# Windowed attention with a soft mixture of experts on one core: the slot logits in four quarters of 64 tokens, some VectorE steps in other forms, and a new table of keys

## The chip, the cores and the metric

The kernel runs on one core of one Trainium2 chip, as one program. The metric is device time in microseconds (us). In three runs the kernel before took 245.77, 247.46 and 247.46 us, so its median is 247.46.

## What is computed

For 4 batches, 8 heads, 768 tokens and 64 features per head, attention keeps the 4 first keys (the sinks) and a window of 128 keys behind each query. Its output, 3072 tokens by 512 features, goes through a soft mixture of 8 experts with 4 slots each:

```
keep = is_sink | in_window                       # n_sink 4, window 128
a = softmax(where(keep, q @ k.T / 8, -1e9)); x = a @ v
logits = x @ phi                                 # [3072, 32]: 32 slots
d = softmax of logits over the 3072 tokens       # dispatch
slot_input = d.T @ x                             # [32, 512]
slot_out[e] = relu(slot_input[e] @ w1[e]) @ w2[e]   # 512 -> 1024 -> 512
c = softmax of logits over the 32 slots          # combine
return c @ slot_out                              # [3072, 512]
```

All data is float32. The weights w1 and w2 are 32 MB, in 32 tiles of 1 MB.

## The kernel before

The attention runs as 12 jobs (`window_path`, L730): 4 batches, each in 3 pieces of 256 tokens (j = 0, 1, 2). A job loads q, k and v, transposes q and k on TensorE (`prep`), and does four softmax tiles (`softmax`, L843): scores on TensorE, row maxima on VectorE (`maxima`), exponentials and row sums on ScalarE (`exps`), then the reciprocal of the sums on VectorE (`inverse`, L901) and the scaling by it on GpSimd, 128x528 elements. The weights are transposed on TensorE, the window's edges are cut by selects on GpSimd (`select`), and `values` multiplies by v. The sinks' weights go another way: they are gathered into `sk`, transposed into `pst`, and added to the logits and to the slot inputs by small matmuls.

At the end of each job `Moe.tokens` (L337) does the dispatch of its 256 tokens, once per job, so 12 times. It is an online softmax over tokens:

- `logits` (L357): 32 slots on 32 partitions, in four column groups of TensorE. Two groups hold the two blocks of 128 tokens, and the other two hold the same two blocks once more. So the tile `L` has 128 partitions and 128 columns; 16 matmuls of 128 columns, and 4 more for the sinks.
- VectorE takes the (negated) maximum of each row into `new`, and the smaller of it and the maximum so far (`tensor_tensor(new, new, old, op=ALU.min)`, L374).
- ScalarE copies the first 64 partitions as they are into `lt`, and the exponentials of the other 64 (L376, L378); their sums go to `zb`. `al`, the factor for what was summed before, is a third small step.
- TensorE turns `lt` by one 128x128 transposition; ScalarE or VectorE copies the two halves out, as `lb` (the weights) and as the logits for the combine.
- `products` (L400) multiplies the weights by the tokens, and `sums` (L419) adds that to `acc`, scaled by `al`. The sinks' part of `acc`, called `far`, has 32 columns per batch; all columns so far are scaled by `al` in each dispatch, by a `tensor_scalar` of 32 to 128 columns, and then the new product is added to the present batch's columns. `totals` (L434) does the same for the sums `z`.

`finish` (L449) joins the maxima of the partition groups, forms the slot inputs `si`, and the tail (`Moe.tail`, L588) does the experts and the combine. `slot_softmax` (L519) prepares the combine's weights once per batch.

What sets the order of the work: each step above is handed to `Plan.add` with a key, an engine and an estimate of its duration; `Plan.order` (L196) lists the steps in an order for each engine, in which the key decides among steps that could start at the same moment. The keys are the sum of 4 times the job's number and an offset from the table `CFG` (L706). The program is then written out in that order, and each engine works through its own list in that order; it is fixed before the run. All DMAs are issued from the one queue of SyncE (SP), in order.

Tiles: `Plan` hands out 4 banks of PSUM for the general tiles named `w`, and 2 larger ones for scores, named `s`. In SBUF there are 24 tiles of 1 MB named `wt` and `first`; 17 of them take weights during the attention, and the others become free for weights only when the attention's last steps have read what is in them. Nearly all instructions are recorded under one line, L156, that of the helper that issues them, so one reads them by the names of their tiles.

The lines to look at: the minimum in a dispatch

```
            plan.add(key, "V", 0.07, lambda e: nc.vector.tensor_tensor(new, new, old, op=ALU.min),
```

the scaling of the far part

```
                    nc.vector.tensor_scalar(far[:, 0:z1], far[:, 0:z1], al, None, op0=ALU.mult)
```

and the step in front of a softmax tile's reciprocal, where `eps` is a tensor

```
            nc.vector.tensor_tensor(z, z, eps, op=ALU.add)
```

Of the kernel before, what the change touches and what calls it, by code (L numbers as in the profile page):

```python
# [8 lines left out]
F32 = mybir.dt.float32  # L9
# [10 lines left out]
P = 128  # L20
# [53 lines left out]
class Sinks:  # L74


    def __init__(self, nc, plan, pool, tmp, c, v, store):
# [3 lines left out]
        self.sk = [pool.tile([P, P], F32, name=f"sk{i}") for i in range(2)]  # L81
# [16 lines left out]
        def clear(e):  # L98
            nc.gpsimd.memset(wide, 0.0)
            nc.gpsimd.memset(self.phi, 0.0)  # L100
            for t in self.sk:
                nc.gpsimd.memset(t, 0.0)
# [20 lines left out]
        plan.add(1.0, "G", 0.6, clear, w=["swide", "vphi", ("sk", 0), ("sk", 1)])  # L123
# [184 lines left out]
class Moe:  # L308
# [6 lines left out]
    def __init__(self, nc, c, keep, work, pools, B):  # L315
# [9 lines left out]
        t = keep.tile([P, 7], F32, name="sums")  # L325
        self.m, self.z, self.zb, self.al = t[:, 0:2], t[:, 2:3], t[:, 3:5], t[:, 5:7]
# [8 lines left out]
        nc.vector.memset(self.z, 0.0)  # L335

    def tokens(self, plan, keys, b, j, x, xn, blocks):  # L337
# [8 lines left out]
        old, new = self.m[:, (n + 1) % 2:(n + 1) % 2 + 1], self.m[:, n % 2:n % 2 + 1]  # L346
# [4 lines left out]
        both = len(blocks) == 2  # L351
# [4 lines left out]

        def logits(e):  # L357
            for a in range(5 if sinks else 4):
                for g in range(4):
                    if a == 4:  # L360
                        nc.tensor.matmul(L["tile"][32 * g:32 * g + 32, 0:P], lhsT=sinks.phi[:, g % 2, :], rhs=sinks.pst,
                                         start=False, stop=True, skip_group_check=True)
                        continue
                    nc.tensor.matmul(L["tile"][32 * g:32 * g + 32, 0:P], lhsT=c.phi[:, a, :],
                                     rhs=xt[:, a, x[g % 2 if both else blocks[0]]], start=(a == 0), stop=(a == 3 and not sinks),
                                     skip_group_check=True)

        plan.add(next(k), "P", 1.16 if sinks else 0.91, logits, r=xs + ["phi"] + (["pst", "vphi"] if sinks else []), w=[L["name"]], new=L, mode=(128, 32))

        key = next(k)  # L370
        plan.add(key, "V", 0.2, lambda e: nc.vector.tensor_reduce(
            new, L["tile"][:, 0:P], op=ALU.max, axis=AX.X, negate=True), r=[L["name"]], w=[("m", n % 2)])
        if n:
            plan.add(key, "V", 0.07, lambda e: nc.vector.tensor_tensor(new, new, old, op=ALU.min),  # L374
                     r=[("m", (n + 1) % 2)], w=[("m", n % 2)])
        plan.add(next(k), "A", 0.16, lambda e: nc.scalar.copy(lt[0:64], L["tile"][0:64, 0:P]), r=[L["name"]], w=["lt0"])  # L376
        plan.add(next(k), "A", 0.48,
                 lambda e: nc.scalar.activation(lt[64:128], L["tile"][64:128, 0:P], AF.Exp, bias=new[64:128],  # L378
                                                accum_out=zb[64:128]),
# [6 lines left out]
        else:  # L386
            next(k)
        plan.add(next(k), "P", 0.11, lambda e: nc.tensor.transpose(T["tile"][:, 0:P], lt, c.ident),
                 r=["lt0", "lt1"], w=[T["name"]], new=T)
        i = slice(0, 2) if both else slice(blocks[0], blocks[0] + 1)  # L390

        def natural(e, w):
            t = T["tile"][:, 0:P].rearrange("p (w i s) -> p w i s", w=2, i=2)
            o, t = (lb, t[:, 1]) if w else (lg[:, i], t[:, 0, i])
            (nc.scalar.copy if e == "A" else nc.vector.tensor_copy)(o, t)
# [4 lines left out]
        def products(e):  # L400
            for g in range(4):
                i, o = g % 2, slice(256 * (g // 2), 256 * (g // 2) + 256)
                if both:
                    lhs, rhs = lb[:, i, :], xn[i][:, o]
                else:
                    rows = slice(64 * i, 64 * i + 64)
                    lhs, rhs = lb[rows, i, :], xn[blocks[0]][rows, o]
# [11 lines left out]
        def sums(e):  # L419
            x, d = acc[:, 0:256], far[:, 32 * b:32 * b + 32]  # L420
            if sinks:
                if n:
# [11 lines left out]
        def totals(e):  # L434
            if not n:
                nc.vector.tensor_copy(z[64:128], zb[64:128])
            elif both:
                nc.vector.scalar_tensor_tensor(z[64:128], z[64:128], al[64:128], zb[64:128],
                                               op0=ALU.mult, op1=ALU.add)
            else:  # L440
                nc.vector.tensor_tensor(z[64:128], z[64:128], al[64:128], op=ALU.mult)
                nc.vector.tensor_tensor(z[64:96], z[64:96], zb[64:96], op=ALU.add)
# [4 lines left out]
        plan.add(key, "V", 0.56 if sinks else 0.4, sums, r=[S["name"], aln], w=["acc"], last=S)  # L447

    def finish(self, plan, keys):  # L449
# [4 lines left out]
        m, mo = self.m[:, (self.n - 1) % 2:(self.n - 1) % 2 + 1], self.m[:, self.n % 2:self.n % 2 + 1]  # L454
        W, Z, SI, D = plan.psum(), plan.psum(), plan.psum(), plan.psum()
        sinks = self.sinks
        f = work.tile([P, 1], F32, name="f")
# [20 lines left out]
        plan.add(next(k), "A", 0.3, lambda e: nc.scalar.activation(f, m, AF.Exp, bias=mo, scale=-1.0), r=mm, w=["f"])  # L478
# [10 lines left out]
        def far(e):  # L489
            nc.tensor.matmul(D["tile"][:, 0:64], lhsT=self.acc[:, 256:384], rhs=s2, start=True, stop=True)  # L490
# [7 lines left out]
        if sinks:  # L498
            key = next(k)
            plan.add(key, "P", 0.2, far, r=["sf", "acc"], w=["sd"], new=D)  # L500
# [18 lines left out]
    def slot_softmax(self, plan, key, b, names):  # L519
# [12 lines left out]
        def sums(_):  # L532
            nc.vector.reduce_sum(rs, e, axis=AX.X)
            nc.vector.tensor_scalar(rs, rs, EPS, None, op0=ALU.add)
            nc.vector.reciprocal(rs, rs)

        plan.add(key, "V", 0.7, sums, w=[n])
# [144 lines left out]
class Weights:  # L682
# [8 lines left out]
    def load(self, t):  # L691
# [3 lines left out]
        else:  # L695
# [10 lines left out]
CFG = {'prep': [12.62, 12.36],  # L706
       'load': [62.54, -93.04],
       'v': [68.49, 63.17],
       'S': -12.9,
       'M': 126.11,  # L710
       'E': 297.18,
       'N': -191.46,
       'K0': 89.87,
       'T': [-201.07, -298.71],
       'K': -214.45,
       'sel': [89.25, -30.52, -145.68, -195.21],
       'val': [295.22, -19.77, 342.69, 369.69],
       'xn': [-57.94],
       'tok': [357.78, -262.56, 29.9, -50.0, 133.69, -75.28, 36.37, -51.64, -299.8, 208.29, -224.86],
       'sm': -143.04,  # L720
       'sinks': -181.93,
       'tr': [63.06, 25.65, 135.89, 140.0, 109.95, 86.26, 129.98, 2.55, 42.1, 2.21, 118.89, 92.88, 82.47, 53.92,
           125.08, 116.73, 96.95, 0.0, 138.66, 84.47, 128.65, 60.63, 120.33, 77.77, 78.14, 114.47, 21.23],
       'w': [105.83, 8.0],
       'fin': [287.49, -10.46, -125.39, -132.28, 35.33, -56.83, -2.84, 389.2, -90.55, 66.83, 472.81],
       'xn1': [40.22],
       'tok1': [-9.5, -16.36, 75.49, -213.58, -107.33, 247.29, -76.98, 179.88, 150.72, 361.93, -107.59]}


def window_path(ctx, tc, c, moe, q, k, v, phi, w1, w2, out):  # L730
# [32 lines left out]
    small = t[:, 1840:1864].rearrange("p (g x y) -> p g x y", g=3, x=2)  # L763
    eps = t[:, 1864:1868]
    qt = fr.tile([P, 4, 256], F32, name="qt")
    nc.vector.memset(eps, EPS)
# [507 lines left out]
```

## Time and profile before

| | us |
|---|---|
| runs, median (lowest, highest) | 247.46 (245.77, 247.46) |
| the profiled execution, device time | 248.19 |
| its span, first to last instruction | 246.5 |
| TensorE busy (matmul) | 212.7 |
| VectorE busy | 168.9 |
| ScalarE busy | 150.4 |
| GpSimd busy | 131.7 |

The profile is one execution, so durations and stretches below are those of the run of 248.19 us; 1.69 us of it lie outside the span, and it is 0.73 us above the median of the three runs. Engines are PE (TensorE's matmuls), PEld (its weight loads), DVE (VectorE), ACT (ScalarE), POOL (GpSimd) and SP (SyncE, which issues the DMAs). A float32 matmul shows as two records. The attention takes about the first 183 us, and its jobs repeat with a period of one batch, about 43 us; the end of the last dispatch and the slot inputs follow up to 194 us, and then the experts and the combine.

### The profile page before, as it was taken

How to read it: one execution, taken by the hardware profiler on the slowest of the kernel's cores; microseconds unless marked ns; L12 is line 12 of the kernel's file. 1: busy time of each engine (PE TensorE's matmuls, PEld its weight loads, DVE VectorE, ACT ScalarE, POOL GpSimd, SP SyncE). 2: the span in 40 equal slices, each digit the busy share in tenths (PEclk: the TensorE clock that was granted, in tenths of full speed). 3: DMA queues.
4: the chain of work that ended last, by engine and by line, in shares of the span. 5: the costliest groups of instructions: out<-in, count | busy, mean ns of one | idle time of the engine just before them, and what ended most of it. 6: DMA issues, size and time to landing. Idle time of an engine off the chain costs nothing.

```text
span 246.5 us, 9008 instructions
## 1 busy us (share of the span) xinstructions
PE 212.7 (86%) x3547; PEld 151.2 (61%) x3547; DVE 168.9 (69%) x455; ACT 150.4 (61%) x579; POOL 131.7 (53%) x247
## 2 busy tenths in 40 slices
PE   7866998998979799798979998898799999998830
PEld 7754676775657577575757766576578533655520
DVE  3387896789999778999956899999736411324240
ACT  2257699758988866898886579888634212123230
POOL 3048687954777785487776646867894160000000
PEclk9979799999999999999979999999999999999995
DMA  5497997788989778998996998983119999999896
GB/s 124 104 212 168 257 212 206 287 186 244 195 251 282 229 256 174 258 198 236 278 263 195 178 274 194 311 268 134 45 44 350 419 366 357 351 349 370 297 314 214
DMA packets 102965, 59.47 MB, mean 241 GB/s; under 512 B 76292, under 2 KB 98820, under 8 KB 102916
## 3 DMA queue, kind: packets, MB, share of 16 engines
q1 hardware_dynamic: 102916, 58.83, 82.9%
q8 instruction: 30, 0.49, 0.8%
q14 instruction: 19, 0.16, 0.2%
HBM read 52.53 MB, written 6.29 MB: 239 GB/s over the span
## 4 chain that ended last, share of the span: by engine, by line
PE 50%; DVE 21%; ACT 14%; DMA 5%; issue 4%; POOL 2%; ACTq 0%; DVEq 0%; POOLq 0%
PE w L156 35%; PE s L156 14%; ACT wt L156 11%; DVE wt L156 8%; DVE s L156 7%; DMA wt<-in_moe_w_dram 5%; DVE sums L156 2%; DVE first L156 2%; PE w L1226 2%; POOL wt L156 1%; DVE acc L156 1%; DVE rs L156 1%; ACT first L156 1%; ACT wt L659 0%; ACT lt L156 0%
## 5 line engine op out<-in xcount | busy, mean ns | idle before, releaser
L156 ACT ACTIVATE wt<-s,wt 128x132 f32<-128x132 f32 x192 | 68.9, 382 | 11.0 <-PE s L156 4.6
L156 POOL TENSOR_TENSOR wt<-wt 128x528 f32<-128x528 f32 x48 | 51.2, 1066 | 28.3 <-DVE wt L156 10.0
L156 POOL TENSOR_SCALAR_AFFINE_SELECT wt<-wt 128x512 f32<-128x512 f32 x88 | 54.0, 639 | 18.8 <-ACT wt L156 12.8
L156 PE MATMUL w<-wt 128*64 128x128 f32 (+2 forms) x548 | 51.3, 324 | 4.3 <-DVE wt L156 2.6
L156 PE MATMUL s<-wt,qt 64*64 64x196 f32 (+2 forms) x768 | 44.4, 332 | 6.7 <-ACT wt L156 5.5
L156 PEld LDWEIGHTS w<-wt 128*64 128x64 f32 (+1 forms) x548 | 37.0, 144 | 16.2 <-POOL wt L156 4.4
L156 ACT ACTIVATION_READ_ACCUMULATOR wt<-s,wt 128x1 f32 x192 | 41.6, 217 | 0.0
L156 ACT COPY wt<-w 128x512 f32<-128x512 f32 (+1 forms) x50 | 28.0, 573 | 12.8 <-PE w L156 9.2
L156 DVE TENSOR_REDUCE wt<-s 128x4 f32<-128x528 f32 x48 | 33.9, 707 | 1.7
L156 PEld LDWEIGHTS s<-wt,qt 64*64 64x64 f32 x768 | 26.0, 135 | 14.3 <-ACT wt L156 7.9
L156 PE MATMUL w<-ident,first 64*128 64x64 f32 x576 | 27.1, 229 | 0.6 <-ACT qt L156 0.2
L156 PEld LDWEIGHTS w<-ident,first 64*128 64x128 f32 x576 | 21.5, 139 | 9.6 <-issue 4.8
L156 PE MATMUL w<-ident,wt 64*128 64x64 f32 (+1 forms) x419 | 24.2, 237 | 3.1 <-POOL wt L156 2.0
L156 PEld LDWEIGHTS w<-ident,wt 64*128 64x128 f32 (+1 forms) x419 | 18.7, 144 | 10.8 <-issue 5.6
L156 DVE COPY first<-w 128x512 f32<-128x512 f32 x28 | 18.8, 678 | 7.2 <-PE w L156 7.2
L156 DVE COPY_PREDICATED s<-later,s 128x256 f32<-128x256 uint8 x48 | 20.2, 421 | 2.1 <-PE s L156 1.1
L156 DVE COPY wt<-w 128x512 f32<-128x512 f32 (+3 forms) x27 | 16.8, 623 | 6.8 <-ACT wt L156 4.3
L156 ACT ACTIVATE qt<-w 128x512 f32<-128x512 f32 (+1 forms) x23 | 13.2, 581 | 9.3 <-PE s L156 7.9
L156 PE MATMUL s<-wt 128*32 128x256 f32 x240 | 15.4, 381 | 0.9 <-DMA wt<-in_moe_w_dram 0.9
L156 ACT COPY first<-w 128x512 f32<-128x512 f32 x20 | 11.6, 605 | 7.0 <-PE w L156 7.0
L156 DVE TENSOR_TENSOR wt<-wt 128x4 f32<-128x4 f32 x48 | 13.6, 284 | 2.2 <-POOL wt L156 1.0
L156 PE MATMUL w<-wt,si 128*32 128x512 f32 x120 | 14.1, 594 | 0.2 <-DVE si L156 0.2
(130 smaller groups left out, 255.9 us busy)
## 6 DMA issues: line engine op xcount, KB each, us to landing
wt<-in_moe_w_dram SPq DMA_DIRECT2D x30, 1024.0 KB, 8.0
wt<-in_v_dram SPq DMA_DIRECT2D x24, 256.0 KB, 4.8
first<-in_q_dram SPq DMA_DIRECT2D x22, 256.0 KB, 3.9
first<-in_k_dram SPq DMA_DIRECT2D x22, 256.0 KB, 4.7
out_dram<-wt SPq DMA_DIRECT2D x4, 1024.0 KB, 8.6
first<-in_moe_w_dram SPq DMA_DIRECT2D x2, 1024.0 KB
out_dram<-wt SPq DMA_DIRECT2D x3, 512.0 KB
first<-in_k_dram SPq DMA_DIRECT2D x4, 128.0 KB, 2.4
```

The costliest lines, as they stand in the source:

```text
L156: return self.tc.keep_in_program_order(f(*args, **kw))
L1226: nc.tensor.matmul(t[:, 0:P], lhsT=c.ident, rhs=c.ident, start=True, stop=True)
```

## The change

- **Logits in quarters.** The four column groups of TensorE now hold four different quarters: the two halves (64 tokens) of the two blocks. The tile `L` has 64 columns. All 128 partitions are copied to the left half of `lt`, and the exponentials of all 128 go to the right half. Because a slot's maximum must be common to the two halves, VectorE copies each half's maximum to the other half's partitions (`met`, two copies of 64x1), and one `tensor_scalar` takes the minimum of own, met and old. The turn is now four transpositions of 64x64. The sinks' `sk` has 64 columns in place of 128.
- **Far part.** It is no longer scaled in each dispatch: a batch's 32 columns are scaled and added by one `scalar_tensor_tensor` while that batch runs, the maxima after each dispatch are kept, and `finish` scales all batches at once on GpSimd by `fb`, with a matmul that exchanges partitions behind it.
- **Small VectorE steps.** `totals`, the minimum, and the additions of EPS are written with one tensor from SBUF. In `inverse` and `slot_softmax` the addition is a `tensor_scalar` over 6 numbers, read as 3 by 2 and written as 2 by 3.
- **Keys.** The table `CFG` has new numbers, and some estimates of duration are new.

```
+                    h, i = divmod(g, 2)
+                    lhs, rhs = (c.phi[:, a, :], xt[:, a, x[i]]) if a < 4 else (sinks.phi[:, i, :], sinks.pst)
+                    nc.tensor.matmul(L["tile"][32 * g:32 * g + 32, 0:64], lhsT=lhs, rhs=rhs[:, quarter[h]],
+                                     start=(a == 0), stop=(a == (4 if sinks else 3)), skip_group_check=True)
...
+        def least(e):
+            for h in range(2):
+                nc.vector.tensor_copy(met[quarter[h]], own[quarter[1 - h]])
+            nc.vector.tensor_scalar(new, own, met, old if n else None, op0=ALU.min, op1=ALU.min if n else ALU.bypass)
...
-                 lambda e: nc.scalar.activation(lt[64:128], L["tile"][64:128, 0:P], AF.Exp, bias=new[64:128],
-                                                accum_out=zb[64:128]),
+                 lambda e: nc.scalar.activation(lt[:, 64:128], L["tile"][:, 0:64], AF.Exp, bias=new, accum_out=zb),
...
-        plan.add(next(k), "P", 0.11, lambda e: nc.tensor.transpose(T["tile"][:, 0:P], lt, c.ident),
+        def turned(e):
+            for w in range(2):
+                for q in quarter:
+                    nc.tensor.matmul(T["tile"][q, 64 * w:64 * w + 64], lhsT=lt[q, 64 * w:64 * w + 64], rhs=c.ident[q, q],
+                                     start=(w == 0), stop=(w == 1), skip_group_check=True)
...
             if sinks:
-                if n:
-                    z1 = 32 * (b + (j > 0))
-                    nc.vector.tensor_scalar(far[:, 0:z1], far[:, 0:z1], al, None, op0=ALU.mult)
                 if j:
-                    nc.vector.tensor_tensor(d, d, S["tile"][:, 256:288], op=ALU.add)
+                    nc.vector.scalar_tensor_tensor(d, d, al, S["tile"][:, 256:288], op0=ALU.mult, op1=ALU.add)
...
+                nc.vector.tensor_scalar(z, z, al, zb, op0=ALU.mult, op1=ALU.add)
...
+            plan.add(key, "G", 0.3, lambda e: nc.gpsimd.tensor_tensor(
+                self.si, self.acc[:, 256:384].rearrange("p (b s) -> p b s", b=self.B),
+                fb.unsqueeze(2).to_broadcast([P, self.B, 32]), op=ALU.mult), r=["f", "acc"], w=["far"])
...
-            nc.vector.tensor_tensor(z, z, eps, op=ALU.add)
+            nc.vector.tensor_scalar(z6.rearrange("p (x y) -> p x y", x=2), z6.rearrange("p (x y) -> p x y", x=3),
+                                    EPS, None, op0=ALU.add)
             nc.vector.reciprocal(z, z)
...
-       'tok': [357.78, -262.56, 29.9, -50.0, 133.69, -75.28, 36.37, -51.64, -299.8, 208.29, -224.86],
+       'tok': [-93.83, -40.26, 115.06, -38.59, 131.06, -79.68, 4.02, 139.77, 195.56, 193.63, 147.41],
```

How the order moves is shown at two places. The first is on PE, at the fourth dispatch (the first job of the second batch), from the logits to the turn, before: `w<-first_77,phi` and `w<-pst,vphi` are the logits, `w<-ident,lt` is the turn, `s<-wt,qt` are scores, the other transpositions have `ident`, and `w<-wt` are values.

```order
L156 MATMUL w<-ident,first_77 128x64 x16
L156 MATMUL w<-first_77,phi 32x128 x16
L156 MATMUL w<-pst,vphi 32x128 x4
L156 MATMUL s<-wt,qt 64x196 x8
L156 MATMUL w<-ident,first_76 128x64 x16
L156 MATMUL s<-wt,qt 64x196 x8
L156 MATMUL w<-ident,wt 128x64 x16
L156 MATMUL w<-ident,sk_164 128x128
L156 MATMUL w<-ident,lt 128x128
```

The same place on PE now:

```order
L155 MATMUL w<-ident,wt 128x64 x16
L155 MATMUL w<-first_77,phi 32x64 x16
L155 MATMUL w<-pst,vphi 32x64 x4
L155 MATMUL s<-wt,qt 64x196 x8
L155 MATMUL w<-ident,first_77 128x64 x16
L155 MATMUL s<-wt,qt 64x196 x8
L155 MATMUL w<-ident,lt 64x64 x4
```

The logits have 64 columns. Three pieces of other work stand between them and the turn, where there were five; the transposition of `first_77` (the tokens, for the products) has moved behind the logits, and those of `wt` and `sk` no longer stand in front of the turn.

On DVE, at the third dispatch, from the maximum of the logits on, before: `sums` holds the small tensors of the dispatch (maxima, factors and sums), `wt<-wt 128x4` are the two steps of `inverse`, and `wt<-s` is a softmax tile's maximum.

```order
L156 TENSOR_REDUCE sums<-w 128x1
L156 TENSOR_TENSOR sums<-sums 128x1
L156 COPY_PREDICATED s<-later,s 128x2x2x64
L156 TENSOR_REDUCE wt<-s 128x2x2
L156 TENSOR_TENSOR wt<-wt 128x4
L156 RECIPROCAL wt<-wt 128x4
L156 SCALAR_TENSOR_TENSOR sums<-sums 64x1
```

The same dispatch on DVE now:

```order
L155 TENSOR_REDUCE sums<-w 128x1
L155 TENSOR_SCALAR wt<-wt 128x6
L155 RECIPROCAL wt<-wt 128x4
L155 COPY sums<-sums 64x1 x2
L155 TENSOR_SCALAR sums<-sums 128x1
L155 COPY first_77<-w 128x8x64 x2
```

Three instructions stand in place of the one minimum, and here an `inverse` has come between the maximum and the minimum. The addition of EPS is in the program as one run of 6 elements, 128x6, like the one over `rs` in `slot_softmax`, which reads 128x6 before and now; the 3 by 2 and the 2 by 3 are not to be seen in it.

## Rows read from the trace of the kernel before

**Rows 1.** The profile's first part: busy time of each engine, its share of the span, and instructions.

```profile
PE 212.7 (86%) x3547; PEld 151.2 (61%) x3547; DVE 168.9 (69%) x455; ACT 150.4 (61%) x579; POOL 131.7 (53%) x247
```

**Rows 2.** Four stretches: from and to, length, then the busy time of each engine with its count of instructions, then the granted clock of TensorE, the mean share of the DMA engines and GB/s. The first two are one batch each; the third is the end of the attention; the fourth is all that follows.

```profile
40.60:83.50 42.90, 38.36 (x734) 28.38 (x734) 37.63 (x96) 35.07 (x141) 29.95 (x52) 1.00 0.86 236
83.50:126.10 42.60, 38.37 (x734) 28.38 (x734) 37.18 (x97) 34.59 (x139) 29.54 (x52) 1.00 0.90 240
...
163.00:182.80 19.80, 17.48 (x333) 12.96 (x327) 15.72 (x41) 14.06 (x61) 16.50 (x29) 1.00 0.36 113
182.80:246.50 63.70, 50.65 (x604) 29.96 (x600) 19.23 (x50) 15.50 (x39) 9.29 (x23) 0.94 0.96 332
```

**Rows 3.** DMA issues from SP's queue in order of time, from 160 us to 220: start, duration of the issuing, queue, operation, destination and source, count.

```profile
162.26 0.54 SPq L156 DMA_DIRECT2D wt<-in_moe_w_dram  x1
...
182.87 2.80 SPq L156 DMA_DIRECT2D wt<-in_moe_w_dram  x4
191.62 0.37 SPq L156 DMA_DIRECT2D first<-in_moe_w_dram  x1
196.08 22.87 SPq L156 DMA_DIRECT2D wt<-in_moe_w_dram  x9
```

**Rows 4.** The chain of work that ended last: its shares of the span by engine, and the longest piece of its last part (start, duration, what).

```profile
PE 50%; DVE 21%; ACT 14%; DMA 5%; issue 4%; POOL 2%; ACTq 0%; DVEq 0%; POOLq 0%
...
216.09 11.39 DMA wt<-in_moe_w_dram
```

**Rows 5.** What PE waited for from 40.6 to 126.1 us, two batches: us in total, times, the longest.

```profile
PE s L156 <- ACT wt L156: 2.7, 4, 0.8
PE w L156 <- DVE wt L156: 1.8, 2, 1.1
PE w L156 <- DVE pst L156: 1.8, 2, 1.2
PE w L156 <- ACT lt L156: 0.7, 2, 0.4
PE w L156 <- ACT wt L156: 0.4, 2, 0.2
PE w L156 <- ACT qt L156: 0.3, 2, 0.2
```

**Rows 6.** PE in order of time: start, duration, operation, destination and operands, tile of the array, shape of one, count, and in brackets the idle time before and what ended it. The first rows are the fourth dispatch, from its logits to its turn; the last two are a dispatch's products with the sinks and the scores that follow.

```profile
77.11 1.08 PE L156 MATMUL w<-first,phi 128*32 128x128 f32 x32
78.01 0.40 PE L156 MATMUL w<-pst,vphi 128*32 128x128 f32 x8
78.34 0.89 PE L156 MATMUL s<-wt,qt 64*64 64x196 f32 x16
...
81.29 0.71 PE L156 MATMUL w<-ident,wt 64*128 64x64 f32 x15 [0.37 <-ACT lt L156]
...
83.51 0.33 PE L156 MATMUL w<-ident,lt 128*128 128x128 f32 x1 [1.21 <-DVE pst L156]
...
86.11 0.26 PE L156 MATMUL w<-sk,lb 128*32 128x32 f32 x8
86.31 0.89 PE L156 MATMUL s<-wt,qt 64*64 64x196 f32 x16
```

**Rows 7.** Groups of instructions by shape over the whole span: line, engine, operation, tiles, shapes, count, then busy us and mean ns of one, then the idle time before them.

```profile
L156 DVE TENSOR_TENSOR wt<-wt 128x4 f32<-128x4 f32 x48 | 13.6, 284 | 2.2 <-POOL wt L156 1.0 <-ACT wt L156 0.9
L156 DVE TENSOR_TENSOR sums<-sums 128x1 f32<-128x1 f32 x11 | 7.2, 659 | 0.4
...
L156 DVE TENSOR_REDUCE sums<-w 128x1 f32<-128x128 f32 x12 | 3.3, 278 | 2.1 <-PE w L156 1.5
...
L156 ACT ACTIVATE lt<-w,sums 64x128 f32<-64x128 f32 x12 | 4.3, 362 | 0.3
...
L156 DVE SCALAR_TENSOR_TENSOR sums<-sums 64x1 f32<-64x1 f32 x11 | 2.4, 219 | 1.2 <-ACT lt L156 0.9
...
L156 DVE TENSOR_SCALAR acc<-acc,sums 128x96 f32<-128x96 f32 x3 | 1.6, 527 | 0.0
...
L156 DVE TENSOR_TENSOR acc<-acc,w 128x32 f32<-128x32 f32 x8 | 1.5, 188 | 1.3 <-PE w L156 0.6
...
L156 DVE TENSOR_SCALAR acc<-acc,sums 128x64 f32<-128x64 f32 x3 | 1.3, 429 | 0.0
...
L156 DVE TENSOR_SCALAR acc<-acc,sums 128x32 f32<-128x32 f32 x3 | 1.3, 422 | 0.0
...
L156 DVE TENSOR_SCALAR acc<-acc,sums 128x128 f32<-128x128 f32 x2 | 1.0, 514 | 0.0
```

**Rows 8.** The addition of EPS over `rs` in `slot_softmax`, four times: shortest, median and longest in ns, first and last start, shape.

```profile
L156 DVE TENSOR_SCALAR rs<-rs x4: 173/968/969, 74.0 to 195.6; 128x6 f32<-128x6 f32 x4
```

**Rows 9.** DVE in order of time at three moments: start, duration, engine, operation, tiles and shapes, count.

```profile
38.75 0.15 DVE L156 COPY sums<-sums 64x1 f32<-64x1 f32 x1
...
122.02 1.04 DVE L156 TENSOR_TENSOR sums<-sums 128x1 f32<-128x1 f32 x1
...
190.31 0.27 DVE L156 TENSOR_SCALAR rz<-sums,f,eps 128x1 f32<-128x1 f32 x1
```

**Rows 10.** POOL in order of time at two of these moments, in the same columns; in brackets the idle time before.

```profile
121.98 1.07 POOL L156 TENSOR_TENSOR wt<-wt 128x528 f32<-128x528 f32 x1 [0.40 <-DVE sums L156]
...
190.31 0.46 POOL L156 TENSOR_TENSOR qt<-call,qt 128x128 fp32r<-128x128 f32 x1
```

More of the change, by code (lines that the diff above doesn't have):

```diff
@@ L100, in clear @@
             nc.gpsimd.memset(self.phi, 0.0)
-            for t in self.sk:
-                nc.gpsimd.memset(t, 0.0)
+            nc.gpsimd.memset(self.pst[64:128], 0.0)
         def selectors(e):
@@ L345, in tokens @@
         n, self.n = self.n, self.n + 1
-        old, new = self.m[:, (n + 1) % 2:(n + 1) % 2 + 1], self.m[:, n % 2:n % 2 + 1]
+        old, new = self.m[:, n - 1:n], self.m[:, n:n + 1]
         lt, z, acc, xt = self.lt, self.z, self.acc, self.xt
@@ L355, in tokens @@
         xs = [("xt", b, u) for b in blocks for u in range(2)]
+        (own, met), quarter = self.own, [slice(64 * h, 64 * h + 64) for h in range(2)]
         def logits(e):
@@ L359, in logits @@
                 for g in range(4):
[L360 to L366, printed above, removed]
@@ new lines, in tokens @@
+        plan.add(next(k), "P", 0.62 if sinks else 0.52, logits, r=xs + ["phi"] + (["pst", "vphi"] if sinks else []), w=[L["name"]], new=L, mode=(128, 32))
+        def least(e):
+            for h in range(2):
+                nc.vector.tensor_copy(met[quarter[h]], own[quarter[1 - h]])
+            nc.vector.tensor_scalar(new, own, met, old if n else None, op0=ALU.min, op1=ALU.min if n else ALU.bypass)
+        key = next(k)
+        plan.add(key, "V", 0.18, lambda e: nc.vector.tensor_reduce(
+            own, L["tile"][:, 0:64], op=ALU.max, axis=AX.X, negate=True), r=[L["name"]], w=["own"])
@@ L380, in tokens @@
+        plan.add(key, "V", 0.25, least, r=["own", ("m", (n + 1) % 2)], w=[("m", n % 2)])
+        plan.add(next(k), "A", 0.12, lambda e: nc.scalar.copy(lt[:, 0:64], L["tile"][:, 0:64]), r=[L["name"]], w=["lt0"])
+        plan.add(next(k), "A", 0.42,
+                 lambda e: nc.scalar.activation(lt[:, 64:128], L["tile"][:, 0:64], AF.Exp, bias=new, accum_out=zb),
                  r=[L["name"], ("m", n % 2)], w=["lt1", zbn], last=L)
@@ L849, in softmax @@
         s = plan.psum("s")
[L850 removed]
+        nm, z, z6 = small[:, g % 3, 0:4], small[:, g % 3, 4:8], small[:, g % 3, 4:10]
         pt = pts[g % PT]
@@ L928, in sinks_transposed @@
         h = plan.psum()
-        add(key, "P", 0.15, lambda e: nc.tensor.transpose(h["tile"][:, 0:P], sinks.sk[n % 2], c.ident),
-            r=[("sk", n % 2)], w=[h["name"]], new=h)
-        add(key, "AV", (0.17, 0.2), lambda e: copy(e, sinks.pst, h["tile"][:, 0:P]), r=[h["name"]], w=["pst"], last=h)
+        add(key, "P", 0.15, lambda e: nc.tensor.transpose(h["tile"][0:64, 0:P], sinks.sk[n % 2], c.ident),
+            r=[("sk", n % 2)], w=[h["name"]], new=h, mode=HALVES)
+        add(key, "AV", (0.17, 0.2), lambda e: copy(e, sinks.pst[0:64], h["tile"][0:64, 0:P]),
+            r=[h["name"]], w=["pst"], last=h)
     def select(key, n, quad, i):
```

107 lines of the change are left out of this document (45 added, 62 removed).

## The prediction, as it was written before the changed kernel ran

> **What bounds the kernel now.** I read the busy times first: PE is busy 86% of the span and DVE 69% [rows 1]. These are averages over two unlike parts, so I took stretches next. One batch of the attention takes 42.7 us, with PE busy 38.4 of it and DVE 37.2 to 37.6, about 90% and 88% [rows 2]. Two engines close to full, handing work to each other, set the period together; ACT (35 of 42.7) comes next. What PE waits for in two batches is 7.7 us in all, in fourteen waits of at most 1.2 us [rows 5]: many small gaps, no single one.
>
> After 182.8 us the picture is another: the DMA engines are busy 96% of the time, while from 163 to 182.8 us they were busy 36% [rows 2]. SP's queue shows why: after 162.26 us no weight is asked for until 182.87, when the last values have been computed and four tiles come free; ten more follow as others come free [rows 3]. The chain that ended last has a weight's transfer of 11.39 us at its end [rows 4]. So from 182.8 us on nearly the same 63.7 us of transfers and matmuls follow whenever the attention ends, and a microsecond taken from the attention is a microsecond at the end. The chain's shares, PE 50% and DVE 21% [rows 4], say that both engines' work counts.
>
> **PE, logits.** In the fourth dispatch the logits start at 77.11 and the next work at 78.34: 1.23 us [rows 6]. The first four fifths, 32 records in sets of four, take 78.01 - 77.11 = 0.90 us, so a set takes 0.1125 and ten sets 1.125; 0.105 is left for starting. With half the columns I halve the sets: 10 x 0.056 + 0.105 = 0.67, a gain of 0.56 us. The trace has no matmuls of 64 columns of this kind, so I bound it. Below, all is halved: 0.62. Above, the products with the sinks, 8 records of 32 columns, take 86.31 - 86.11 = 0.20, or 0.025 each; 40 records at that rate take 1.0 and gain 0.23. I take 0.67, since ten sets spaced by their own columns is what rows 6 show at 128. The turn in four pieces: 15 transpositions of 64x64 take 0.71, 0.047 each [rows 6], so four take 0.19 beside 0.33 for the one. PE's list lets the next piece begin before the end of such a row, so I count nothing there, and 0.1 either way.
>
> **DVE, per dispatch.** It loses the maximum over 128 columns (0.278), the old minimum (0.659), `totals` (0.219), and the scaling of the far part: 1.6 + 1.3 + 1.3 + 1.0 = 5.2 us in 11 dispatches, with 1.5 of additions 0.61 each [rows 7]; together 1.77 us. Why does a minimum of 128x1 cost 0.659? At 122.02 one takes 1.04 us, and POOL's scaling, begun at 121.98, ends just then [rows 9, 10]: DVE stood until POOL's instruction ended. It gains: the maximum over 64 columns, 0.21 (between 0.278 and the 0.15 of a step with next to no elements); two copies of 64x1 at 0.15 [rows 9]; the new minimum and `totals`, each a `tensor_scalar` of 128x1 at 0.27, the row at 190.31, which ended at 190.58 while POOL's instruction of the same start ran to 190.77, so it did not stand [rows 9, 10]; and 8 steps of 128x32 in 11 dispatches, at 0.21 between 0.188 and 0.219 [rows 7], 0.15 each. Together 0.21 + 0.30 + 0.27 + 0.27 + 0.15 = 1.20. The gain is 0.57 us. If the copies too had to stand as the `rs` rows do (0.968 [rows 8]), they would cost 1.94 in place of 0.30, and DVE would lose 1.1 per dispatch; I take the 0.15, because the nearest row that was taken beside POOL, that at 190.31, was not held.
>
> **DVE, the addition of EPS.** The 48 additions in `inverse` take 284 ns on the mean [rows 7]. The new form is in the program as one run of 128x6 from and to SBUF. The trace has that very form: the one over `rs`, which takes 173 ns once and 968 or 969 otherwise [rows 8]. The short one is the last, at 195.6, when POOL has nothing to do. So a run of six waits for POOL as the two tensors did, and I cost this edit at nothing, in `inverse` and in `slot_softmax`. The ends: if it never waits, 48 x (284 - 173) = 5.3 us of DVE less; if it waits at twice as many places, 5.3 more.
>
> A rule of the Trainium skill bears on this. "SBUF — State Buffer", § Who interferes with whom, says that a `tensor_scalar` can run in a mode that takes the port pair DVE shares with GpSimd, and that the later of the two then stands until the earlier has ended; "VectorE: DVE Perf Modes", § Mode 2×_2P, makes an even outermost dimension, or an odd one that is equal on both sides, the condition. Read 3 by 2 and written 2 by 3, the six would escape it; as one run of six they would not, and the rows of `rs` agree. By the escape the forecast would be that of the fourth case below.
>
> **Others.** ACT copies and exponentiates 64 columns on 128 partitions in place of 128 columns on 64: shorter by half a step's columns, hidden behind ACT's slack of 8 us a batch. SP's issues are of the same number and sizes. `finish` gets a multiplication on POOL between the last sum and the slot inputs: 0.46, as for 128x128 at 190.31 [rows 10], and about 0.1 for the hand-over, 0.6 in all, on the path to the tail. If POOL were still at other work it would be more; at 190.77 it is at its end.
>
> **The sum.** PE's work per dispatch falls by 0.56 and DVE's by 0.57, so the two that set the period shrink alike, and with the same gaps the period shrinks by 0.55: 12 x 0.55 = 6.6 us, less 0.6 in `finish`: 6.0. From the profiled 248.19 that is 242.2. That execution is 0.73 above the median of the runs, so the forecast is 241.5. Its own range is 239 to 244.5: the low end has the logits at 0.62 and a few of the gaps of rows 5 gone; the high end has them at 1.0, where PE gains 0.23 and DVE 0.57 and I count half the sum, 12 x 0.4 = 4.8, less 0.6 and 1 for new gaps.
>
> **What is late next.** The turn waits for `lt`, which waits for the minimum. Between logits and turn PE now has scores, transpositions and scores, by rows 6 about 0.89 + 0.71 + 0.89, less what they overlap: 2.3 us. The path needs 0.21 + 0.30 + 0.27 = 0.78 on DVE, then on ACT 0.36 for the exponentials [rows 7] and about as much again for the copy and the factor beside them, and 0.3 for hand-overs: 1.8. So 0.5 us of cover is left.
>
> **Rivals.**
>
> 1. *Slower: the turn waits for DVE.* With three instructions in place of one, the minimum has more that can be late; at the third dispatch an addition of EPS stands between maximum and copies, and that can stand 0.97 for POOL [rows 8]. If in the two dispatches of each batch with the short cover (8 in all) DVE is late by that and by one more softmax maximum, about 1.1, PE waits 0.97 + 1.1 - 0.5 = 1.6 us, 12.8 us in all: 241.5 + 12.8 = 254. It undoes the gain from 6.0 / 8 = 0.75 per turn, and makes the kernel slower by 1% from 8.4 / 8 = 1.05. For it: today's turn waits 1.21 at 83.51 [rows 6]. Against: that wait was for a copy of `pst`, and no longer stands there.
> 2. *No change.* DVE stands for POOL elsewhere by as much as it saves, or the transfers in the attention (DMA share 0.86 to 0.90 [rows 2]) hold jobs back as they get shorter: about 247. Against the latter, 20 us at 36% are free before 182.8.
> 3. *More: the gaps go too.* The waits for `pst` and `lt` are 2.5 of the 7.7 us [rows 5]; with the new order and the shorter path they may end, and half of the others with them: 3.5 to 5 us over all batches, 237 to 238.
> 4. *The addition of EPS does escape POOL.* Then 5.3 us of DVE go besides; PE is then the one that sets the period, and of the 0.44 a dispatch DVE's share of the chain counts, 21% [rows 4]: 12 x 0.44 x 0.21 = 1.1 us, or up to twice that, about 240.
>
> **How the numbers follow.** The forecast gets 0.53, the first rival 0.12, the second 0.16, the third 0.12 and the fourth 0.07. About 1% is what runs of this kernel can tell from no change, below 245.0 or above 249.9. Faster: the third and fourth, and nearly all of the forecast, 0.71; the same: the second and a bit of the forecast, 0.18; slower: most of the first, 0.11. The range is to leave out the first case and the lowest end of the third: 237.0 to 247.5, wider than the forecast's own 239 to 244.5.
>
> **What would show it.** Right: each dispatch's logits taking 0.6 to 0.75 us from their start to the next work; the minimum's `tensor_scalar` of 128x1 near 0.2 to 0.3 also beside POOL; the 128x6 additions long beside POOL and 0.17 without it, their mean within 0.1 of 284; a batch in 40.5 to 41.5 us; the jump to the last weights' issue at 176 to 178 in place of 182.87, with some 63.7 us behind it. Wrong: logits of 1 us; a wait of the turn over 1 us in most batches; 128x6 additions all at 0.17; or a stretch behind the last values that is longer than before.

## The result and the profile after

The changed kernel took 234.36 us (median of four runs, 232.99 to 239.74) beside 246.62 for the kernel before in the same group of runs: 0.9493 times, 95% interval [0.9385, 0.9601]. Some executions of a kernel here come out slower as a whole at a lower TensorE clock (the one of 239.74, at 0.945); the ratios, here and below, are of means without them, so they differ a little from those of the medians. Once more, in a later group, it was 0.9474 [0.9396, 0.9553]. The forecast was 241.5, and the time lies below its range of 237.0 to 247.5. The profiled execution took 232.99.

Busy times over the span, which answer to [rows 1]:

```profile
PE 203.3 (88%) x3633; PEld 146.8 (63%) x3633; DVE 152.6 (66%) x454; ACT 148.2 (64%) x593; POOL 132.4 (57%) x247
```

Two batches and the stretch behind the last values, in the columns of [rows 2]:

```profile
72.45:109.72 37.27, 35.97 (x756) 27.40 (x756) 31.98 (x96) 34.09 (x143) 29.67 (x52) 1.00 1.02 264
109.72:147.94 38.22, 36.21 (x756) 27.53 (x756) 32.07 (x96) 34.28 (x143) 29.63 (x52) 1.00 0.94 247
...
168.50:231.30 62.80, 50.16 (x613) 30.09 (x613) 19.45 (x52) 14.47 (x37) 9.18 (x22) 0.95 0.97 337
```

A batch takes 37.3 to 38.2 us in place of 42.7. PE stands still for 1.3 to 2.0 us of it (length less busy time) where it was 4.2 to 4.5, and DVE is busy 32 in place of 37.4. The end part, 62.8 us, is 0.9 shorter. SP's queue, against [rows 3]:

```profile
168.50 2.77 SPq L155 DMA_DIRECT2D wt<-in_moe_w_dram  x4
175.56 0.37 SPq L155 DMA_DIRECT2D first<-in_moe_w_dram  x1
182.20 20.84 SPq L155 DMA_DIRECT2D wt<-in_moe_w_dram  x9
```

Four weights at once are asked for 14.4 us earlier than at 182.87, and the span is 15.2 us shorter: nearly all the gain lies in the attention, and the tail follows.

PE in order of time in the fourth dispatch, which answers to [rows 6]:

```profile
72.45 0.65 PE L155 MATMUL w<-first,phi 128*32 128x64 f32 x32
72.92 0.29 PE L155 MATMUL w<-pst,vphi 128*32 128x64 f32 x8
73.14 0.90 PE L155 MATMUL s<-wt,qt 64*64 64x196 f32 x16
73.97 0.71 PE L155 MATMUL w<-ident,first 64*128 64x64 f32 x16
74.61 0.89 PE L155 MATMUL s<-wt,qt 64*64 64x196 f32 x16
75.33 0.41 PE L155 MATMUL w<-ident,lt 64*64 64x64 f32 x8
75.67 1.96 PE L155 MATMUL w<-wt 128*64 128x256 f32 x24
77.56 0.71 PE L155 MATMUL w<-ident,wt 64*128 64x64 f32 x16
78.20 0.30 PE L155 MATMUL w<-ident,sk 128*64 128x128 f32 x1
78.43 0.89 PE L155 MATMUL s<-wt,qt 64*64 64x196 f32 x16
79.25 0.71 PE L155 MATMUL w<-ident,first 64*128 64x64 f32 x16
79.90 0.66 PE L155 MATMUL w<-first,lb 128*32 128x256 f32 x8
```

No wait is left. The logits take 73.14 - 72.45 = 0.69 us, the turn 0.34. In the kernel before the transposition of `sk` stood right before the turn, which then waited 1.21 us for the copy of `pst` [rows 6], and one piece of work lay between turn and products; now `sk` stands behind the turn, and five pieces lie between the turn and the products, 4.2 us.

PE's products and turns over three batches, from the logits of the first dispatch to those of the tenth, with the idle time before them in the last column, for the kernel before (35.35 to 164.01 us) and then for the changed one (35.29 to 147.94):

```profile
L156 PE MATMUL w<-first,lb 128*32 128x256 f32 x72 | 6.0, 397 | 0.0
L156 PE MATMUL w<-ident,lt 128*128 128x128 f32 x9 | 3.0, 329 | 3.6 <-DVE pst L156 3.0 <-ACT wt L156 0.6
```

```profile
L155 PE MATMUL w<-first,lb 128*32 128x256 f32 x72 | 5.9, 391 | 0.6 <-ACT wt L155 0.6
L155 PE MATMUL w<-ident,lt 64*64 64x64 f32 x72 | 4.5, 224 | 0.0
```

All of PE's gaps in them fall from 12.2 us to 5.1. The turns wait 3.6 us before and not at all now. The products hardly wait in either. The waits of the scores for ACT fall from 4.1 to 2.0, and the values wait 1.2 for POOL in place of 2.6 for DVE.

DVE's groups by shape, against [rows 7]:

```profile
L155 DVE TENSOR_SCALAR wt<-wt 128x6 f32<-128x6 f32 x48 | 11.2, 233 | 1.3 <-ACT wt L155 1.3
...
L155 DVE TENSOR_SCALAR sums<-sums 128x1 f32<-128x1 f32 x23 | 6.1, 264 | 0.4
...
L155 DVE COPY sums<-sums 64x1 f32<-64x1 f32 x24 | 3.6, 148 | 0.6
L155 DVE TENSOR_REDUCE sums<-w 128x1 f32<-128x64 f32 x12 | 2.6, 218 | 0.8 <-PE w L155 0.7
```

### The profile page after: what moved, and what is told of

Read it like the earlier page. It is cut to its first block, busy times and chain, and to the rows that moved or that the text cites. A ratio compares the mean times of both kernels' runs of the same rounds, so it can differ in the third digit from the quotient of the medians.

```text
span 231.3 us, 9132 instructions
## 1 busy us (share of the span) xinstructions
PE 203.3 (88%) x3633; PEld 146.8 (63%) x3633; DVE 152.6 (66%) x454; ACT 148.2 (64%) x593; POOL 132.4 (57%) x247
## 4 chain that ended last, share of the span: by engine, by line
PE 63%; DVE 10%; POOL 9%; ACT 8%; issue 6%; POOLq 0%; ACTq 0%; DVEq 0%
PE w L155 42%; PE s L155 19%; POOL wt L155 8%; DVE wt L155 4%; ACT wt L155 4%; DVE s L155 2%; PE w L1226 2%; ACT qt L155 2%; DVE sums L155 1%; ACT wt L658 1%; POOL sk L155 0%; DVE wt L643 0%; POOL vphi L155 0%; ACT pst L155 0%; DVE phi L155 0%
## 5 line engine op out<-in xcount | busy, mean ns | idle before, releaser
L155 PE MATMUL w<-wt 128*64 128x128 f32 (+2 forms) x548 | 49.8, 316 | 3.5 <-POOL wt L155 2.0
L155 PE MATMUL s<-wt,qt 64*64 64x196 f32 (+2 forms) x768 | 45.1, 337 | 5.7 <-ACT wt L155 3.6
L155 PEld LDWEIGHTS w<-wt 128*64 128x64 f32 (+1 forms) x548 | 35.5, 140 | 16.6 <-POOL wt L155 4.8
L155 ACT ACTIVATION_READ_ACCUMULATOR wt<-s,wt 128x1 f32 x192 | 39.9, 208 | 0.0
L155 ACT COPY wt<-w 128x512 f32<-128x512 f32 (+1 forms) x44 | 25.0, 575 | 10.1 <-PE w L155 9.0
L155 DVE COPY wt<-w 128x512 f32<-128x512 f32 (+3 forms) x33 | 20.9, 634 | 13.6 <-PE w L155 7.7
L155 ACT COPY first<-w 128x512 f32<-128x512 f32 x33 | 19.1, 591 | 12.9 <-PE w L155 12.5
L155 PE MATMUL w<-ident,wt 64*128 64x64 f32 (+1 forms) x419 | 23.4, 235 | 2.7 <-POOL wt L155 1.5
L155 DVE TENSOR_SCALAR wt<-wt 128x6 f32<-128x6 f32 x48 | 11.2, 233 | 1.3 <-ACT wt L155 1.3
L155 PEld LDWEIGHTS s<-wt 128*32 128x32 f32 x240 | 7.8, 110 | 5.8 <-issue 0.8
```

Of the source, the lines that this page charges most:

```text
L155: return self.tc.keep_in_program_order(f(*args, **kw))
```

## Experiments

Theory 1: the new instructions are worth what I summed, and the new keys bring the rest. Theory 2: shorter work closes PE's gaps by itself. Ratios are to the kernel before in the same group of runs.

**The old keys under the new instructions** (the table `CFG` of the kernel before, nothing else).

> The changed kernel, all its instructions, with the table of keys of the kernel before. Theory 1: 240 to 243, a batch of 40 to 41.5 us, and DVE busy 34 to 36 of it, because the instructions that stand for POOL and the copies come back to DVE. Theory 2: 234 to 236.5, a batch of 37.3 to 38.

241.42 us, 0.9756 [0.9679, 0.9833]. Two batches, and SP's last issues in the attention:

```profile
34.02:75.71 41.69, 37.81 (x775) 28.15 (x772) 35.33 (x102) 33.68 (x137) 31.12 (x55) 1.00 0.89 245
75.71:118.72 43.01, 38.55 (x776) 28.25 (x772) 37.01 (x107) 34.04 (x142) 31.49 (x54) 1.00 0.96 256
```

```profile
178.12 2.58 SPq L155 DMA_DIRECT2D wt<-in_moe_w_dram  x4
```

This is the forecast: the time (241.5), the batch (41.3 us over three), the sum of PE's gaps (4.3 us a batch), the issue at 178.12 (176 to 178). Theory 1 holds; some 7 us come from the keys.

They are not the same gaps, though. With the new steps the old keys give another list than that of the kernel before: in the first five dispatches the products stand right behind the turn, where the kernel before has one piece of work. Over three batches these products wait 3.5 us and the turns 1.2, in place of 0.0 and 3.6.

**The new keys under the old instructions.**

> The kernel before, all its instructions, with the table of keys of the changed kernel. Theory 1 in its strong form (the new order is better for either kernel): 240 to 242. In its weak form (the new order only suits the new work): 245 to 250. Theory 2: 246 to 248, no gain. Only a time near 241 tells the theories apart here; the busy time of DVE in a batch tells besides whether the order alone takes standing time and copies from it (theory 1: 33 to 35 us instead of 37.4).

292.98 us, 1.1836 [1.1762, 1.191], far beyond all three ranges. The table suits only the new work. One batch shows why a poor order can cost twice:

```profile
73.85:139.22 65.37, 51.77 (x689) 35.82 (x687) 35.51 (x90) 29.94 (x117) 25.63 (x45) 0.74 0.82 230
```

PE waits 13.6 us, and the clock granted to it falls to 0.74 on the mean, so that its work is longer too.

**The removals one by one in the old order.** The minimum: `tensor_scalar(new, new, old, None, op0=ALU.min)` in place of the `tensor_tensor`. The far part: the `tensor_scalar` by `al` left out. The logits: `[..., 0:64]` in place of `0:P`, both halves read from it. Then all three.

> The kernel before with one edit: the old value of the running minimum comes in as a scalar operand, so that the instruction has one tensor in SBUF. The order stays. If the 0.659 us are standing for POOL, each of the 11 falls to 0.2 to 0.3 us, DVE loses about 4 us over the kernel. Theory 1: in the old order DVE's share of the chain, a fifth, counts, so 245 to 246.5. Theory 2: the relief closes gaps of PE, 242 to 244.

> The kernel before without the scaling of the far part (which is left out: the far sums are not rescaled), 11 instructions of DVE with a mean of 0.47 us, 5.2 us; the order stays. If DVE's time counts in full in the old order, as the minimum's did (4.9 us of standing away, 4.6 us of time), 242 to 243.5; by DVE's share of the chain, 21%, 245.5 to 246.5.

> The kernel before with the logits of 64 of a block's 128 tokens computed and read twice (half of the logits are left out); the order stays. PE's 40 matmuls have 64 columns in place of 128 and take 0.56 us less, 12 times 6.7. If PE's time counts in full: 240 to 241. If the gaps widen by as much because DVE sets the period: 245 to 247.

> The kernel before with three removals in its old order and with its old keys: the running minimum takes the old value as a scalar operand, the far part is not scaled, and of each dispatch's two halves only 64 of 128 tokens' logits are computed and read twice (half of the logits and the far scaling are left out). PE and DVE lose about what the change takes from them, the order stays. Theory 1 (the order brings the half that I missed): about the sum that I predicted, 240 to 242.5, and the gaps of PE in a batch stay near 4 us. Theory 2 (shorter work closes the gaps by itself, whatever the order): 234 to 236.5, gaps near 1.5 us.

| edit | us | ratio, interval | taken away |
|---|---|---|---|
| minimum | 242.65 | 0.9795 [0.9734, 0.9856] | DVE 4.8 us |
| far part | 242.73 | 0.9797 [0.9738, 0.9856] | DVE 5.2 us |
| logits | 247.85 | 0.9969 [0.9919, 1.0019] | PE 1.5 us a batch, 6 in all |
| all three | 238.83 | 0.9624 [0.9554, 0.9693] | all |

DVE's group of the minimum in the first of them, against 7.2 us and 659 ns in [rows 7]:

```profile
L156 DVE TENSOR_SCALAR sums<-sums 128x1 f32<-128x1 f32 x11 | 2.4, 214 | 0.4
```

In the old order DVE's time counts in full (about 5 us for 5), and PE's little (0.8 us for 6). A part of that is the clock: nine of the ten runs with half the logits had a mean granted clock of 0.94 to 0.95. The tenth, at 0.973, took 244.51, and the kernel before took 245.79 to 246.92 at 0.973 and 0.974, so at the same clock PE's 6 us bring 1.3 to 2.4. One batch at full clock and one below it, from an execution of 248.41 us, in the columns of [rows 2]:

```profile
75.41:120.17 44.76, 39.58 (x739) 28.67 (x735) 36.59 (x98) 34.59 (x138) 29.62 (x51) 0.92 0.86 227
120.17:162.23 42.06, 36.85 (x739) 27.06 (x735) 36.56 (x98) 34.53 (x138) 29.55 (x51) 1.00 0.93 252
```

At full clock PE's work is shorter by 1.5 us than in [rows 2], and its gap grows from between 4.2 and 4.5 us to 5.2; in the other batch the lower clock takes what is left. Over three batches PE's gaps are 12.2 us in the kernel before, 11.1 without the old minimum, 8.5 without the scaling, 14.7 with half the logits and 10.3 with all three, whose time lies between the two theories' ranges. So theory 2 falls for PE and holds in part for DVE.

**What the keys bring: the share of the copies between DVE and ACT (1a) or the places of the instructions (1b).** 193 copies may be done by DVE or ACT; the plan gives 63 to DVE with the new keys, 80 with the old. First I moved some by hand: `qt` and `pst` to DVE in the new order, to ACT in the old.

> The changed kernel, in its own order at every place, but the copies of the scaled queries (qt) and of pst are all done by VectorE instead of mostly by ScalarE. DVE gains eight copies of about 0.69 us and ten of 0.28, some 8 us in all, ACT loses them. If the new keys win by sharing the copies better between the two engines (1a), this gives back 3 us or more: 237 to 240. If they win by the places of the instructions alone (1b), 234 to 236.

> The changed kernel with the table of keys of the kernel before, in that order at every place, but the copies of the scaled queries (qt) and of pst all done by ScalarE. DVE loses eight copies of 0.69 and seven of 0.28, 7.4 us in all, and stands as low as in the changed kernel. 1a (the share of the copies): 235 to 238.5 against the 241.4 with the copies on DVE. 1b (the places): 240.5 to 243.

244.72 us, 0.99 [0.9841, 0.9959], and 242.24 us, 0.9798 [0.9739, 0.9857]. The first moved more than I had counted, 23 copies of `qt` and not eight, and gives most of the gain back, beyond both ranges; the second brings nothing, as 1b had it. Then the whole cross: the places of one plan (the order list), with the engines of the other (`order = [(t, x, i, share[i]) for t, x, i, _ in order]`).

> The changed kernel with the old keys, in that order at every place, but each of the 193 copies that either engine may do is given to the engine that does it in the changed kernel: DVE has 63 of them in place of 80. Share (1a): DVE stands near 32 us a batch and the time follows, 236 to 238.5. Places (1b): 240 to 243, as with the old share, though DVE has less to do.

> The reverse: the changed kernel with its new keys, in its own order at every place, but each of the 193 copies on the engine that does it with the old keys (80 on DVE in place of 63). Share (1a): 239 to 242, DVE near 35 us a batch. Places (1b): 234 to 236. If both this and the reverse run come out near 241, share and places only help together.

Old places with the new share: 252.43 us, 1.0291 [1.0179, 1.0402]. New places with the old share: 235.49 us, 0.9578 [0.9488, 0.9669]. The second is what 1b foretold. The first lies beyond both ranges: DVE has less to do, 33.8 us a batch, and the time is 11 us above that with the old share. So the new share alone brings nothing, and it is the places (1b), with a share that suits them. The last of three batches of the second run, and the sum of the three:

```profile
110.89:149.94 39.05, 36.11 (x756) 27.35 (x756) 35.04 (x102) 32.26 (x137) 29.61 (x51) 1.00 0.95 245
sum 116.61, PE 107.95 PEld 81.63 DVE 103.93 ACT 97.28 POOL 88.86; mean PE 35.98 PEld 27.21 DVE 34.64 ACT 32.43 POOL 29.62
```

DVE is nearly as busy as with the old keys (34.6 a batch, 35.1 there), and the time is 1.8% lower all the same, with intervals that don't meet. In the new places the share is worth another 1.0%, which the intervals don't separate from nothing. PE's products and turns over these three batches, with the idle time before them in the last column, for the old keys and then for the new places with the old share:

```profile
L155 PE MATMUL w<-first,lb 128*32 128x256 f32 x72 | 6.0, 390 | 3.5 <-DVE call L155 2.8 <-ACT lb L155 0.6
L155 PE MATMUL w<-ident,lt 64*64 64x64 f32 x72 | 4.2, 229 | 1.2 <-ACT wt L155 1.0
```

```profile
L155 PE MATMUL w<-first,lb 128*32 128x256 f32 x72 | 5.9, 391 | 0.6 <-ACT wt L155 0.6
L155 PE MATMUL w<-ident,lt 64*64 64x64 f32 x72 | 4.5, 224 | 0.0
```

These waits fall by 4.1 us, and all of PE's gaps by as much, from 12.8 to 8.7: the others, taken together, stay.

**Which places.** With the old keys PE goes from the turn straight to the products:

```profile
80.33 0.71 PE L155 MATMUL w<-ident,wt 64*128 64x64 f32 x16
81.12 0.45 PE L155 MATMUL w<-ident,lt 64*64 64x64 f32 x8
82.51 0.66 PE L155 MATMUL w<-first,lb 128*32 128x256 f32 x8 [0.95 <-DVE call L155]
```

The work that stands there in the new order I call the cover. It is what the new keys brought (2a), or it is not (2b). I took it away in the new order, built it in the old one, and gave the old table one new row and the new table one old row. In the first, the copy of `lb` and the products follow the turn at once, and take from `sk` what is there at that point.

> The changed kernel with its new keys, but in all dispatches the copy of lb and the products follow the turn at once, as most do with the old keys; the three to five pieces of other work that PE has there now come behind them. If the new keys win by this cover (2a), PE waits 0.3 to 1 us before the products again, 12 times: 238 to 244. If the cover there is not what counts (2b), 234 to 236.

> The changed kernel with the old keys (241.4 us), but where the products follow the turn at once the next piece of PE's list (scores or transpositions, about 0.8 us) is put between them; that is in the first five dispatches. 2a: the waits before these products (0.95, 0.31, 0.95, 0.95 and 0.31 us, 3.5 in all) go, 237.5 to 239.5. 2b: 240.5 to 243.

> The changed kernel with the old keys (241.4 us) but for one row, the eleven keys of a dispatch's own steps ('tok'), which are the new ones. By it one to three pieces of PE's other work (0.7 to 3 us) come between each turn and its products, where the old row had none in six dispatches. 2a (the cover between turn and products is what the new keys brought): the waits of 0.95 and 0.31 us before the products go, 3.5 us over nine dispatches, 236.5 to 239. 2b: 240 to 243, or slower, because the rest of the table no longer suits.

> The changed kernel with its new keys but for one row, that of the transpositions of k and q ('prep'), which is the old one. Then in four of the first five dispatches only one or two pieces of work stand between turn and products, in the later ones three to five as before. 2a: where a single 0.7 us piece is left the products wait some 0.3 us, in all 1 to 2 us more, and scores that come earlier wait for ACT: 236 to 239. 2b: 234 to 235.5.

Cover taken away: 250.88 us, 1.0166 [1.0066, 1.0267], 17 us more than the changed kernel beside it (234.02):

```profile
117.34:161.28 43.94, 39.96 (x755) 29.89 (x756) 31.64 (x96) 34.63 (x143) 29.70 (x52) 0.92 0.87 221
```

The engines have the same work, DVE as little as in the changed kernel. PE's gaps are back at 4.0 us, and at the lower clock its own work takes nearly 4 us more. The time lies beyond both ranges, and the edit takes away more than the cover, for it also moves the copy of `lb` up in the list of ACT or DVE. The products wait 3.4 us over three batches, as with the old keys, and other work of PE waits 7.5 for ACT, where it was 2.6 in the changed kernel. Cover built by hand: 248.06, 1.0015 [0.996, 1.007], slower than either range. The products no longer wait, but the scores put before them do, for ACT to free their bank; with the row `tok`, 241.88, 0.9782 [0.9727, 0.9837], as 2b had it, the products don't wait either, but the turn does, behind a transposition of `sk` right before it. One line of each:

```profile
41.96 0.89 PE L155 MATMUL s<-wt,qt 64*64 64x196 f32 x16 [1.57 <-ACT wt L155]
```

```profile
39.84 0.45 PE L155 MATMUL w<-ident,lt 64*64 64x64 f32 x8 [1.20 <-DVE pst L155]
```

With the old row `prep` in the new table: 239.55, 0.9697 [0.9638, 0.9756], just above the range of 2a. Its first batch is longer, the later ones are not, and of that batch's gaps of 5.7 us the products' wait is 0.4:

```profile
33.48:77.22 43.74, 38.07 (x772) 28.46 (x772) 33.11 (x97) 35.85 (x142) 30.08 (x54) 1.00 0.94 259
77.22:114.92 37.70, 35.59 (x743) 26.86 (x739) 31.62 (x94) 32.94 (x140) 29.39 (x50) 1.00 0.97 251
```

So products right behind the turn wait, in either order, and the cover ends that; alone it is not enough, for each local step handed the wait on. How much of the 17 us is the cover and how much the moved copies is not shown.

**What sets the period in the new order.** The minimum from two SBUF tensors again; the EPS addition with gaps between its rows (`tensor_scalar(zo, zi, EPS, None, op0=ALU.add)`, `zi` 3 by 2 of pitch 3, `zo` 2 by 3 of pitch 4); the logits' first four sets done twice.

> The changed kernel with the running minimum taken from two SBUF tensors again (a scalar_tensor_tensor of the same 128x1, in the same place, in 11 of 12 dispatches). If such an instruction stands for POOL in the new order too, its mean goes from 0.26 to some 0.6 us. Where DVE still is on the path, the time goes up by most of 11 x 0.35 = 3.9, to 236 to 238.5; where DVE has slack by now (84% busy), by under 1, 234 to 235.5.

> The changed kernel with the six sums of EPS laid out with gaps, so that the addition cannot be made one run of six: it reads 3 by 2 and writes 2 by 3, and the reciprocal reads the result. If the odd outermost dimension keeps it out of POOL's way, the 48 additions fall from 0.233 to about 0.17 us with none over 0.3; DVE loses 3 us, and the time 0 to 1.5: 233 to 234.5. If not, the mean stays at 0.23 or more and the time at 234 to 235.

> The changed kernel with the first four of the five sets of logit matmuls done twice in each dispatch (the second pass starts the sums anew, so the result stays). PE gets 32 matmuls of 64 columns more, about 0.47 us, 12 times: 5.6 us. If PE sets the period in the new order, as its 96% of a batch say, the time goes up by 4 to 6: 238 to 240. If DVE or the handing over still set it, by less than 2.

> The changed kernel once more, on the chip of this group of runs, so that the others can be set against it: 233 to 236.

| edit | us | ratio, interval | added |
|---|---|---|---|
| none | 234.02 | 0.9474 [0.9396, 0.9553] | |
| minimum | 234.86 | 0.9454 [0.9387, 0.9521] | DVE 1.7 us |
| EPS | 233.01 | 0.9384 [0.9321, 0.9447] | DVE -3.4 us |
| logits | 238.55 | 0.9625 [0.9528, 0.9722] | PE 1.15 us a batch, 4.6 in all |

The minimum stands for POOL again in some places (0.43 us on the mean, no more than 0.58). The EPS additions by shortest, median and longest, in the changed kernel and with the gaps:

```profile
L155 DVE TENSOR_SCALAR wt<-wt x48: 159/162/648, 15.2 to 162.4; 128x6 f32<-128x6 f32 x48
```

```profile
L155 DVE TENSOR_SCALAR wt<-wt x48: 144/149/161, 14.7 to 162.4; 128x6 f32<-128x6 f32 x48
```

In the changed kernel twelve of the 48 start when a POOL instruction has 0.2 us or more to go, and each ends within 0.03 us of that one's end. With the gaps ten start so, and none is held: the additions take 4.0 us less in all, the reciprocals, of six elements now, 0.6 more. The time is 1% lower, and the intervals overlap. PE's 4.6 us cost 3.7 (1.5% of 247), though that interval too overlaps the other's. In the new order it is PE that counts more, as its 36.0 of 37.3 us in a batch and the chain's shares, against [rows 4], say:

```profile
PE 63%; DVE 10%; POOL 9%; ACT 8%; issue 6%; POOLq 0%; ACTq 0%; DVEq 0%
```

The version with the gaps is the fastest that I ran; that it beats the changed kernel is not shown.

## Why the prediction missed

- **The step that failed** is "with the same gaps the period shrinks by 0.55". PE's gaps, 4.1 us a batch over three, stay as long in sum with the old keys (4.3 us, 241.42 us in all) and fall to 1.7 with the new, which is 7 us. The third rival had named this, at 237 to 238 and with 0.12, but its price doesn't follow from its rows: the 2.5 us for `pst` and `lt` and half of the other 5.2 are 5.1 us in two batches, so about 10 in four, and 241.5 less 10 is 231 to 232. It put down 3.5 to 5 for all batches.
- **Where it could have been seen.** The first rival notes that the wait of 1.21 us for `pst` "no longer stands there", since `sk` has moved away from in front of the turn; the sum takes no gain from it. Over three batches that wait was 3.0 us, and it went. "What is late next" weighed the cover between logits and turn, and stopped there. The hand-over behind it, from turn to products, has one piece of work in each dispatch of the kernel before, three to five in the first ten of the changed kernel, and none in five with the old keys, where it waits.
- **What was right.** Logits 0.69 us (0.67 expected); the turn 0.34 beside 0.33, though not for the reason given (the 15 of [rows 6] are records, two to a transposition, so four take 0.38 by that row and not 0.19); the minimum and `totals` 0.264 (0.27), also beside POOL; copies 0.148 (0.15); maximum 0.218 (0.21); the EPS additions held as one run of six, mean 233 ns, within 0.1 us of 284; 62.8 us behind the last values (63.7). The four additions over `rs` were costed at nothing, and in the new order none is held (172 ns on the mean, 770 before). DVE's gain with the old keys is 36.88 - 35.14 = 1.74 us a batch over three, and three times 0.57 is 1.71.
- **Right by luck.** "The two that set the period shrink alike" made the sum indifferent to which of them counts. In the old order it is DVE above all: PE's 6 us were worth 0.8, at the same clock 1.3 to 2.4, the minimum's 4.8 about 5. Had only the logits been cut, the same reasoning would have failed.
- **The rivals.** No turn waits for DVE in the steady batches (first rival), and nothing else took the gain (second). On the fourth, the addition does escape POOL once it cannot be made one run: all 48 take 144 to 161 ns. "VectorE: DVE Perf Modes", § Mode 2×_2P, of the Trainium skill asks for an outermost dimension that is even, or odd and equal on both sides, for the mode with two ports; 3 by 2 read and 2 by 3 written is neither, and the 48 additions agree.
- **Open** is how much of the 7 us each place brings. Neither the row `tok` nor the cover alone, in the order of the old keys, brings any.

## What to carry to other kernels

When a change brings a new order along, run the new work in the old order (and the old engines at the new places) before putting the gain down to either. The old table is not the old order: with new steps it gives a third list, with waits of its own. Before predicting, list for every hand-over what the waiting engine has in between, in the old and the new order, and not for the one that waits today alone. That two engines are both close to full doesn't say that both count: take time from each by itself.

## What I had not expected of the hardware

A wait of TensorE can be followed by a loss larger than itself. In the run without the cover PE's instructions were those of the changed kernel. Its three batches had gaps of 4.4, 4.2 and 4.0 us and mean granted clocks of 1.00, 0.96 and 0.92, and PE's own time in the last was 40 us in place of 36; in the run with the new keys on the old work the clock was 0.74 in a batch with 13.6 us of gaps. It is not a rule of these runs: with the old keys PE's gaps were as long, and its clock stayed at 1.00 in all three batches. The kernel before shows both cases on the same work, the values behind a turn that had waited 1.21 us:

```profile
83.77 1.96 PE L156 MATMUL w<-wt 128*64 128x256 f32 x24
126.39 3.48 PE L156 MATMUL w<-wt 128*64 128x256 f32 x24
```

In the first the granted clock is 1.00 throughout. In the second it is 0.50 from 126.7 us on (1.2 in place of 2.4 GHz), and the work takes 1.5 us longer. What decides between the two is not shown.
